# A fused attention + two-MLP kernel: the small products of each tile gathered behind h, scores three tiles ahead, and one weight conversion moved to a later stage

## Chip, cores, metric

The kernel runs on one core of one Trainium2 chip. The metric is the device time of one execution in microseconds; smaller is better. TensorE is called PE here, its weight loads PEld, VectorE DVE, ScalarE ACT, GpSimd POOL, and the queue from which most transfers are issued SP.

## Reference

All inputs are float64 or float32 arrays; the output is float32, 4608 x 512.

```python
# attention in chunks of 64 tokens, 8 heads of 64, 4608 tokens in all
attn = softmax(q_c @ k_c.T / 8)            # per chunk and head, 64 x 64
x = attn @ v_c                             # -> [4608, 512]
# first MLP, d_ff 1024
h = x @ w_in
sm = softmax(h)
solu = h * sm
ln = (solu - mean(solu)) / sqrt(var(solu) + 1e-6) * g_ln
y = ln @ w_out                             # -> [4608, 512]
# second MLP, d_ff 1536
g, val = y @ w_gate, y @ w_val
out = (g * sigmoid(g) * val) @ w_out2
```

## The kernel before

The weights arrive as float64 and are turned into float32 pairs (high and low part) on the chip, by a chain called here a conversion: `conv_a` (ACT takes the magnitude from the upper words), `conv_r` (ACT scales the lower words), `clamp` (POOL), `conv_b` (two DVE operations on the bits) and `conv_c` (POOL adds). Products with float32 accuracy are three passes over such pairs.

The program is three stages behind each other on PE.

**Attention and h (the slots).** The 4608 tokens are 36 tiles of 128. Slot t of `for t in range(NT): slot(t)` computes the 24 matmuls of `hidden(t)` (h = x @ w_in for tile t, 128x512 each, tile `h` in PSUM), in six blocks of four called `h(0)` to `h(5)`. Between the blocks stand the steps of neighbouring tiles: `scores(t + 2)` and `pv(t + 1)` (32 small 64x64 matmuls each by the profile's count, both into the PSUM tile `so_ps`), `p_transpose(t + 1)` (4 transposes into `pt` and an ACT copy), `x_split(t + 1)` (ACT writes the high part of x, DVE the low part), the softmax steps `s_*`, the softmax and normalisation over h of tile t - 1 (`ln_max`, `ln_exp`, `ln_mul`, `ln_sq`), and of tile t - 2 `ln_norm` on POOL and `ln_T` (8 transposes into `tr`, ACT copies, a store to DRAM). Everything is written in program order; each engine works through its own instructions in that order, and a waiting instruction holds up all behind it on its engine. `wo_step(t, i)` fits conversions in: w_out is 8 units and w_out2 is 12, and unit u begins in slot u * 5 // 3, so 20 units lie in 36 slots. Its load is issued at the end of one slot, and its `conv_a`, `conv_r` and `clamp` stand in the next slot, the clamp ahead of `ln_norm` on POOL. `l_load` and `l_split` fetch the normalised tiles back for the next stage.

**y.** `y_run` multiplies by w_out, while `w_tick` converts w_gate and w_val.

**Gate/value products and the last product.** 72 calls of `step(s, f)`, each 42 matmuls of 128x384 (seven products into the PSUM tiles pa to pd), with ACT, DVE and POOL combining the results, then the product with w_out2, whose converted float32 form was stored in `wo_dram` and is read by `t_load`.

Of the kernel before, what the change touches and what calls it, by code (L numbers as in the profile page):

```python
# [8 lines left out]
F32 = mybir.dt.float32  # L9
# [3 lines left out]
I64 = mybir.dt.int64  # L13
# [4 lines left out]
P = 128  # L18
# [5 lines left out]
def attn_moe_moe2_kernel(  # L24
# [13 lines left out]
    nc = tc.nc  # L38
    NT = qT.shape[0]
# [6 lines left out]
    KF = DF // P  # L46
    FT = w_gate.shape[0]
# [66 lines left out]
    def conv_b(cs):  # L114

        for c in cs:
            shift(c)
        for c in cs:
            sign(c)
        return cs  # L120

    def conv_c(c, out=None):

        m, words = c
        if out is None:
# [9 lines left out]
        c, f = divmod(u, KF // 2)  # L135
        return 2 * f, slice(c * DM // 2, (c + 1) * DM // 2)

    def split_scaled(wB, u, w):

        f0, cols = wo_unit(u)  # L140
        for j in range(2):
            f, x = f0 + j, w[:, j * DM // 2:(j + 1) * DM // 2]
            g, hi, lo = g_sb[:, f:f + 1], wB[:, f, 0, cols], wB[:, f, 1, cols]
            nc.scalar.activation(out=hi, in_=x, func=AF.Copy, scale=g)
            nc.vector.scalar_tensor_tensor(
                out=lo, in0=x, scalar=g, in1=hi.bitcast(F32), op0=ALU.mult, op1=ALU.subtract
            )
# [5 lines left out]
    NY = 3 * KF  # L153
# [79 lines left out]
    with ExitStack() as ph1:  # L233
# [92 lines left out]
        def p_transpose(t):  # L326
            e = st.pop(t).rearrange("p (n c) j -> p n (c j)", c=2)
            pt = ps_t.tile([P, H, CH], F32, tag="t", name="pt")
            for n in range(NP):
                nc.tensor.transpose(pt[:, 2 * n:2 * n + 2].rearrange("p h i -> p (h i)"), e[:, n], ident)  # L330
            p = att.tile([P, H, CH], F32, tag="p", name="p")
# [175 lines left out]
        def shf(k):  # L507
            shift(ca[k])
# [50 lines left out]
        add(3)  # L559
        clp(POOL, 4)  # L560
        p_transpose(0)
        scores(1)
        shf(4)
        rnd(4)
# [27 lines left out]
        clp(POOL, 7)  # L592
        add(6)
        p_transpose(1)
        shf(7)
        rnd(7)
        high(6)
# [15 lines left out]
        raws, cs, lows = {}, {}, {}

        NCV = KF + FT
        cv_at = [u * 5 // 3 for u in range(NCV)]

        def wo_step(t, i):

            for u in range(NCV):  # L620
                if cv_at[u] + i != t:
                    continue
                if i == 0:
                    raws[u] = wo_raw(u) if u < KF else raw_load(stage, w_out2[u - KF])
                elif i == 1:
                    cs[u] = conv_a(stage, raws.pop(u))
                    conv_r(cs[u])
                    clamp(nc.gpsimd, cs[u])
                elif i == 2:
                    conv_b([cs[u]])  # L630
                    conv_c(cs[u])
                elif u < KF:
                    split_scaled(wB, u, cs.pop(u)[0])
                else:
                    nc.sync.dma_start(out=wo_dram[u - KF], in_=cs.pop(u)[0])

        def slot(t):


            S = NH // 6  # L640
            new, nxt, old, out = (
                x if 0 <= x < NT else None for x in (t + 2, t + 1 if t else NT, t - 1, t - 2)
            )
            do = lambda x, *fns: [fn(x) for fn in fns if x is not None]
            h = lambda i: t and hidden(t, i * S, (i + 1) * S)
            h(0)
            if t in lows:
                lows.pop(t)()
            h(1)
            do(old, ln_exp)  # L650
            do(new, scores)
            do(nxt, p_transpose)
            do(new, s_max)
            h(2)
            wo_step(t, 1)
            do(out, ln_norm)
            do(old, ln_rec)
            do(new, s_sub)
            do(old, ln_mul)
            h(3)  # L660
            do(new, s_exp)
            if nxt is not None:
# [6 lines left out]
            h(4)  # L669
            do(new, s_rec)  # L670
            do(old, ln_sq)
            wo_step(t, 3)
            h(5)
# [10 lines left out]
            if t in (NT - 3, NT - 2):  # L684
                l_split()

        lraw, lsplit = [], []

# [31 lines left out]
        ln_norm(t - 1)  # L720
# [23 lines left out]
    with ExitStack() as ph2:  # L744
# [200 lines left out]
        def t_load(p):  # L945
# [3 lines left out]
            for j, dst in enumerate((x[:, 1:8:6], x[:, 2:7:4])):  # L949
                nc.sync.dma_start(  # L950
                    out=dst, in_=wo_dram[2 * p + j].rearrange("p (b n) -> p b n", b=2)
                )

        def t_sums(p):
# [61 lines left out]
        for s in range(NSG):  # L1016
            for n, f in enumerate([*range(RING, FT), *range(RING)] if s == 0 else range(FT)):
                late = n + FT * (s - NSG + 2)
                if s == 0 and n in (2, 4, 6):
                    cache_load(n // 2 - 1)  # L1020
                if s + 1 < NSG:
                    if n == (s == 0):
                        y_load(s + 1)
                    if n == (4 if s == 0 else 1):
                        todo = y_units(s + 1)
                if late == 7:
                    t_load(0)
                    t_load(1)
                if 8 <= late < 8 + 2 * NFP and late % 2 == 0:
                    t_sums(late // 2 - 4)  # L1030
                if late in (20, 21):
                    x_load(late - 20)
                step(s, f)
                k = -(-len(todo) // ((FT if s < NSG - 2 else 7) - n)) if todo else 0
                for x in todo[:k]:
                    x()
                todo = todo[k:]
                if 8 <= late < 8 + 2 * NFP and late % 2:
                    t_split(late // 2 - 4)
# [100 lines left out]
```

## Time and profile before

| | us |
|---|---|
| median of 3 runs | 1446.99 (1446.33 to 1447.7) |
| profiled execution, its own time | 1449.33 |
| its span, first to last instruction | 1447.5 |
| PE busy | 1340.7 (93%) |
| DVE, ACT, POOL busy | 978.8 (68%), 625.5 (43%), 429.6 (30%) |

A row of the timeline gives the start, the time covered, the engine, the line, the operation with its output and inputs, the count, and in brackets the idle time of the engine just before with what ended it. "PEclk 1.00" is the full granted clock of PE, 2.4 GHz; 0.5 would be 1.2 GHz. Matmuls overlap, so the modelled end of one run lies a little behind the start of the next.

### The profile page before, as it was taken

To read this page: it belongs to the slowest core of one execution; us is meant where nothing else is said; L and a number is where in the kernel's file an instruction comes from. 1 tells how busy PE (TensorE), PEld (TensorE's weight loads), DVE (VectorE), ACT (ScalarE), POOL (GpSimd) and SP (SyncE) were. 2 spreads that over 40 slices of the span, in tenths; PEclk is the share of its full clock that TensorE was granted. 3 is DMA by queue.
4 is the path that set the end of the run, shared out by engine and by line. 5 is a ranking of instruction groups with operands and counts; after the bars stand their busy time and mean duration, and the time that the engine had idled before them with its cause. 6 is when DMAs were issued, how large, how long until landed. Compare 5 with 4: busy or idle time off the path is not lost.

```text
span 1447.5 us, 26121 instructions
## 1 busy us (share of the span) xinstructions
PE 1340.7 (93%) x10054; PEld 1264.6 (87%) x10054; DVE 978.8 (68%) x1648; ACT 625.5 (43%) x1000; POOL 429.6 (30%) x578
## 2 busy tenths in 40 slices
PE   4888788878889999999999999999999999999998
PEld 3666666666669999999999999999999989999998
DVE  6767656555553777756776676766777777888775
ACT  5556555544455655533333333333333324333342
POOL 5435434434442344412222221322333101100011
PEclk9999999988999999999999999999999999999999
DMA  5544454545646899989738678585899744444441
GB/s 196 161 139 140 157 164 140 155 155 164 194 140 237 338 358 372 330 332 422 272 118 307 247 257 313 195 304 208 321 329 338 251 145 139 148 135 143 132 133 72
DMA packets 143085, 318.39 MB, mean 220 GB/s; under 512 B 10864, under 2 KB 90736, under 8 KB 135280
## 3 DMA queue, kind: packets, MB, share of 16 engines
q1 hardware_dynamic: 136624, 308.06, 61.3%
q10 hardware_dynamic: 6336, 8.65, 1.7%
q8 instruction: 79, 1.29, 0.4%
q14 instruction: 46, 0.38, 0.1%
HBM read 225.45 MB, written 91.23 MB: 219 GB/s over the span
## 4 chain that ended last, share of the span: by engine, by line
PE 75%; DMA 8%; DVE 5%; POOL 4%; issue 4%; ACT 3%; SPq 1%; POOLq 0%; ACTq 0%; DVEq 0%
PE y L164 14%; PE pa L888 10%; PE pd L888 10%; PE pc L888 9%; PE opa L1068 5%; PE opc L1068 5%; PE opb L1068 5%; PE h L372 5%; DMA raw<-in_moe_w_out 5%; PE pb L888 5%; PE tr L453 3%; PE opd L1068 3%; POOL so L441 2%; DVE nm L383 1%; PE so_ps L260 1%
## 5 line engine op out<-in xcount | busy, mean ns | idle before, releaser
L372 PE MATMUL h<-wA,x 128*128 128x512 f32 x864 | 234.5, 422 | 6.3 <-DVE se L395 3.5
L372 PEld LDWEIGHTS h<-wA,x 128*128 128x128 f32 x864 | 169.5, 204 | 43.5 <-DVE se L395 4.2
L164 PE MATMUL y<-lnT,wB 128*128 128x384 f32 x1152 | 201.7, 336 | 0.0
L164 PEld LDWEIGHTS y<-lnT,wB 128*128 128x128 f32 x1152 | 201.2, 189 | 0.0
L921 POOL TENSOR_TENSOR u<-u,p 128x384 f32<-128x384 f32 x72 | 73.1, 1016 | 398.8 <-DVE u L920 391.2
L923 ACT ACTIVATE u<-pa 128x384 f32<-128x384 f32 x72 | 35.5, 492 | 175.3 <-PE pa L888 142.6
L1078 POOL TENSOR_TENSOR work<-work 128x256 f32<-128x256 f32 x36 | 26.4, 744 | 255.6 <-DVE work L1078 255.6
L453 PE MATMUL tr<-ident,so 128*128 128x128 f32 x288 | 47.5, 318 | 56.7 <-POOL so L441 56.7
L453 PEld LDWEIGHTS tr<-ident,so 128*128 128x128 f32 x288 | 37.7, 162 | 61.0 <-POOL so L441 59.7
L383 DVE TENSOR_REDUCE nm<-h 128x1 f32<-128x1024 f32 x36 | 43.9, 1220 | 65.1 <-PE h L372 65.1
L924 DVE TENSOR_TENSOR u<-pa,u 128x384 f32<-128x384 f32 x72 | 40.1, 557 | 70.3 <-ACT u L923 70.2
L1004 ACT ACTIVATE hl<-ry 128x1792 fp32r<-128x1792 f32 x28 | 47.6, 1704 | 78.2 <-PE opd L1068 53.3
L95 POOL TENSOR_SCALAR m<-m 128x512 f32<-128x512 f32 x44 | 38.0, 864 | 140.8 <-ACT m L82 140.8
L928 ACT ACTIVATE u<-p 128x384 f32<-128x384 f32 x72 | 37.9, 526 | 96.7 <-DVE p L927 96.7
L1004 ACT ACTIVATE hl<-work 128x1792 fp32r<-128x1792 f32 x26 | 44.3, 1705 | 80.6 <-PE opd L1068 53.3
L707 DVE TENSOR_TENSOR lnT<-lr,lnT 128x1536 fp32r<-128x1536 f32 x24 | 47.7, 1987 | 39.7 <-ACT lnT L706 36.7
L888 PE MATMUL pd<-ykb,ws 128*128 128x384 f32 x360 | 72.3, 335 | 1.4 <-DVE u L920 1.4
L888 PE MATMUL pa<-ykb,ws 128*128 128x384 f32 x360 | 72.2, 334 | 0.4 <-ACT p L913 0.4
L888 PE MATMUL pc<-ykb,ws 128*128 128x384 f32 x360 | 72.1, 334 | 0.0
L1009 DVE TENSOR_TENSOR hl<-ry,hl 128x1792 fp32r<-128x1792 f32 x28 | 56.5, 2022 | 17.5 <-ACT hl L1004 17.4
L390 ACT ACTIVATE eh<-h,nm 128x1024 f32<-128x1024 f32 x36 | 40.1, 1115 | 62.9 <-DVE nm L383 62.9
L888 PE MATMUL pa<-yka,ws 128*128 128x384 f32 x324 | 65.2, 335 | 1.6 <-ACT p L913 1.6
(141 smaller groups left out, 3247.5 us busy)
## 6 DMA issues: line engine op xcount, KB each, us to landing
ws<-ws SPq DMA_DIRECT2D x57, 1792.0 KB, 8.8
u<-u SPq DMA_DIRECT2D x72, 384.0 KB, 6.8
ln<-lt SPq DMA_DIRECT2D x72, 256.0 KB, 2.7
lr<-ln SPq DMA_DIRECT2D x24, 768.0 KB, 7.2
ry<-u SPq DMA_DIRECT2D x56, 256.0 KB, 3.2
work<-u SPq DMA_DIRECT2D x52, 256.0 KB, 3.2
ws<-shi SPq DMA_DIRECT2D x12, 896.0 KB, 9.9
raw<-in_moe_w_out SPq DMA_DIRECT2D x20, 512.0 KB, 5.0
```

What stands on the lines that cost most here:

```text
L164: nc.tensor.matmul(ys[u], lhsT=wB[:, f, a, d * P:(d + 1) * P], rhs=lnT[m][:, b, f, :], start=(n == 0), stop=(n == NY - 1),)
L372: nc.tensor.matmul(h[:, n * DM:(n + 1) * DM], lhsT=x[:, a, k, :], rhs=wA[:, n * KD + k, b, :], start=(j == 0), stop=(j == NH // 2 - 1),)
L383: nc.vector.tensor_reduce(out=nm, in_=h, axis=AX.X, op=ALU.max, negate=True)
L390: nc.scalar.activation(out=e, in_=h, func=AF.Exp, bias=nm, accum_out=se)
L453: nc.tensor.transpose(tr[:, f, :], so[:, c0:c0 + P], ident)
L707: nc.vector.tensor_tensor(out=lo, in0=x, in1=hi.bitcast(F32), op=ALU.subtract)
L888: nc.tensor.matmul(ps, lhsT=w[:, a, kk * P:(kk + 1) * P], rhs=y[:, b, kk], start=(first and n == 0), stop=(n == 5), skip_group_check=True,)
L921: nc.gpsimd.tensor_tensor(out=u3, in0=u3, in1=p5, op=ALU.add)
L924: nc.vector.tensor_tensor(out=sa, in0=psA, in1=sa, op=ALU.mult)
L1004: nc.scalar.activation(out=hl[n][:, 0], in_=xs[n][:, 1:8], func=AF.Copy)
L1009: nc.vector.tensor_tensor(out=hl[n][:, 1], in0=xs.pop(n)[:, 1:8], in1=hl[n][:, 0].bitcast(F32), op=ALU.subtract,)
L1068: nc.tensor.matmul(acc[g, i, t][:, half], lhsT=hl[n][:, a, j, i * P:(i + 1) * P], rhs=tw[p][:, j, b], start=(p == x == half == 0), stop=(p ...
```

## The change

A slot keeps its work and gets another order. `scores` runs three tiles ahead (`ahead`, t + 3) in place of two, and stands with `pv` and `ln_T` in one block behind `h(5)`; only the 4 transposes of `p_transpose` stay inside h, behind `h(1)`. The ACT copy of `p_transpose` becomes a step of its own (`p_copy`). `ln_max`, `ln_rs` and the low part of x move to other places. w_out's 8 units begin every fourth slot, and the magnitude step stands two slots behind the load. The 12 units of w_out2 leave the slots: as 24 half units of 128x256 they run beside the first 51 calls of `step`. (`NCV` in the diff is `KF + FT`, 20, and `cv_at[u]` is `u * 5 // 3`.)

```diff
 def wo_step(t, name):
-    for u in range(NCV):
-        if cv_at[u] + i != t:
+    for u in range(KF):
+        if t - 4 * u != {"load": 0, "mag": 2, "clamp": 3, "bits": 4, "add": 4, "high": 6, "low": 6}[name]:
             continue
...
 def slot(t):
+    ahead, new, nxt, old, out = at(t + 3), at(t + 2), at(t + 1), at(t - 1), at(t - 2)
+    if t == 0:
+        scores(2)
+        load_qk(4)
+        nxt = None
     h(0)
-    if t in lows:
-        lows.pop(t)()
+    do(nxt, s_mul)
+    do(out, ln_rs)
+    do(old, ln_max)
     h(1)
-    do(old, ln_exp)
-    do(new, scores)
+    do(out, ln_norm)
+    do(new, s_max)
     do(nxt, p_transpose)
-    do(new, s_max)
     h(2)
-    wo_step(t, 1)
-    do(out, ln_norm)
-    do(old, ln_rec)
+    do(old, ln_exp)
     do(new, s_sub)
-    do(old, ln_mul)
+    do(nxt, p_copy)
+    wo_step(t, "bits")
     h(3)
     do(new, s_exp)
-    if nxt is not None:
-        pv(nxt)
-        lows[nxt] = x_split(nxt)
-    do(out, ln_T)
-    wo_step(t, 2)
-    do(old, ln_mu)
-    do(new, s_sum)
+    do(old, ln_rec)
     h(4)
-    do(new, s_rec)
-    do(old, ln_sq)
-    wo_step(t, 3)
+    wo_step(t, "high")
+    do(old, ln_mul)
+    do(new, s_sum)
+    wo_step(t, "clamp")
     h(5)
-    do(new, s_mul)
-    ln_max(t)
-    do(old, ln_rs)
-    if t + 4 < NT:
-        load_qk(t + 4)
-    if t + 3 < NT:
-        load_v(t + 3)
-    wo_step(t, 0)
+    do(nxt, pv)
+    do(new, s_rec)
+    do(old, ln_mu)
+    wo_step(t, "low")
+    if t in (NT - 3, NT - 1):
+        l_split()
+    wo_step(t, "mag")
+    do(ahead, scores)
+    if nxt is not None:
+        x_split(nxt)()
+    do(out, ln_T)
+    do(old, ln_sq)
+    wo_step(t, "add")
+    do(at(t + 5), load_qk)
+    do(at(t + 3), load_v)
+    wo_step(t, "load")
...
 # behind the slots, t = NT - 1
+ln_rs(t - 1)
+ln_max(t)
+ln_norm(t - 1)
 ln_exp(t)
+y_run(wB, 0, NY // 2, ps_h, p2p, ("h",))
...
-ln_T(t - 1)
-y_run(wB, 0, NY, ps_h, p2p, ("h",))
+ln_T(t - 1)
...
 l_split()
+y_run(wB, NY // 2, NY, ps_h, p2p, ("h",))
...
 # gate/value products: 24 half units of w_out2, G = n + FT * s
+if G % 2 == 0 and 0 <= G // 2 - 2 < 2 * FT:
+    v_store(G // 2 - 2)
 step(s, f)
+if G % 2 and 0 <= G // 2 - 1 < 2 * FT:
+    v_bits(G // 2 - 1)
+if G % 2 == 0 and 0 <= G // 2 - 1 < 2 * FT:
+    v_mag(G // 2 - 1)
+if G % 2 and G // 2 < 2 * FT:
+    v_load(G // 2)
```

`v_load` is one SP transfer of 256 KB into `vraw`, `v_mag` is `conv_a`, `conv_r` and `clamp` into `vm`, `v_bits` is `conv_b` and `conv_c`, and `v_store` sends 128 KB to `wo_dram`.

On PE, in the middle of the slots, one slot of before reads as follows, from one slot's h to the next (`so_ps<-kt,qt` are scores, `so_ps<-p,vt` are pv).

```order
L372 MATMUL h<-wA,x 128x512 x16
L260 MATMUL so_ps<-kt,qt 64x64 x16
L330 MATMUL pt<-ident,e 128x128 x4
L372 MATMUL h<-wA,x 128x512 x8
L260 MATMUL so_ps<-p,vt 64x64 x16
L453 MATMUL tr<-ident,so 128x128 x8
L372 MATMUL h<-wA,x 128x512 x16
```

The same place in the changed kernel:

```order
L381 MATMUL h<-wA,x 128x512 x8
L335 MATMUL pt<-ident,e 128x128 x4
L381 MATMUL h<-wA,x 128x512 x16
L265 MATMUL so_ps<-p,vt 64x64 x16
L265 MATMUL so_ps<-kt,qt 64x64 x16
L462 MATMUL tr<-ident,so 128x128 x8
L381 MATMUL h<-wA,x 128x512 x8
```

The instructions of a slot are the same; h is cut once in place of twice (the 16 of before are the last 8 of one tile and the first 8 of the next), and the two 64x64 products now stand next to each other.

On ACT, a slot of before with a conversion reads from the exponential over h (`eh,se`) to the copies of `tr`; `m` and `raw` are the conversion.

```order
L390 ACTIVATE eh,se<-h,nm 128x1024
L332 ACTIVATE p<-pt 128x512
L82 ACTIVATE m<-raw 128x512
L88 ACTIVATE raw<-raw 128x512
L295 ACTIVATE e<-e 128x512
L352 ACTIVATE x<-so_ps 128x512
L455 ACTIVATE lt<-tr 128x512 x2
L419 ACTIVATE eh,sq<-so,nmu 128x1024
```

In the changed kernel a slot with the most conversion work on ACT reads:

```order
L399 ACTIVATE eh,se<-h,nm 128x1024
L341 ACTIVATE p<-pt 128x512
L300 ACTIVATE e<-e 128x512
L146 ACTIVATE wB<-m,g_sb 128x256 x2
L82 ACTIVATE m<-raw 128x512
L88 ACTIVATE raw<-raw 128x512
L361 ACTIVATE x<-so_ps 128x512
L464 ACTIVATE lt<-tr 128x512 x2
L428 ACTIVATE eh,sq<-so,nmu 128x1024
```

The conversion still stands ahead of the high part of x (`x<-so_ps`), but the raw block that it reads was asked for two slots earlier, and the clamp on POOL that follows it stands behind the next slot's `ln_norm`.

In the gate/value products, ACT of the changed kernel reads, at the end of a step with a magnitude and the start of the next (`u<-pa` and `u<-p` are the two sigmoids, `p<-pa` frees the first product's PSUM tile for the fifth):

```order
L939 ACTIVATE u<-pa 128x384
L944 ACTIVATE u<-p_7646 128x384
L82 ACTIVATE vm<-vraw 128x256
L88 ACTIVATE vraw<-vraw 128x256
L820 ACTIVATE ykb<-ry 128x384 x2
L929 ACTIVATE p_7671<-pa 128x384
```

The two new ACT instructions stand between the last sigmoid of one step and the first copy of the next.

## Rows read from the trace of the kernel before

**Rows 1.** Busy time by stretch (us, busy and count per engine, PEclk, DMA, GB/s).

```profile
49.00:425.50 376.50, 307.55 (x3298) 242.79 (x3297) 229.92 (x456) 204.70 (x360) 169.24 (x310) 0.93 0.49 151
...
440.00:631.80 191.80, 191.80 (x1110) 191.80 (x1109) 128.53 (x155) 108.55 (x155) 70.15 (x56) 1.00 0.90 338
631.80:1163.00 531.20, 527.83 (x3036) 524.99 (x3035) 368.18 (x659) 184.04 (x368) 136.77 (x136) 1.00 0.77 278
```

**Rows 2.** Timeline of PE: one whole slot, then the end of the next.

```profile
221.18 3.92 PE L372 MATMUL h<-wA,x 128*128 128x512 f32 x16
225.20 0.69 PE L260 MATMUL so_ps<-kt,qt 64*64 64x64 f32 x32
...
226.24 2.09 PE L372 MATMUL h<-wA,x 128*128 128x512 f32 x8
228.26 0.69 PE L260 MATMUL so_ps<-p,vt 64*64 64x64 f32 x32
228.88 1.09 PE L453 MATMUL tr<-ident,so 128*128 128x128 f32 x8
229.73 3.91 PE L372 MATMUL h<-wA,x 128*128 128x512 f32 x16
...
241.22 1.09 PE L453 MATMUL tr<-ident,so 128*128 128x128 f32 x8 [3.75 <-POOL so L441]
242.07 5.51 PE L372 MATMUL h<-wA,x 128*128 128x512 f32 x16
```

**Rows 3.** All engines in the slot of rows 2 (columns as in rows 1).

```profile
223.42:232.00 8.58, 8.48 (x102) 6.72 (x101) 7.18 (x15) 5.20 (x9) 4.32 (x9) 1.00 0.50 157
```

**Rows 4.** Timeline of PE: slot 2 begins; the last h; behind it.

```profile
48.26 2.09 PE L372 MATMUL h<-wA,x 128*128 128x512 f32 x8 [0.56 <-ACT x L352]
...
423.42 2.11 PE L372 MATMUL h<-wA,x 128*128 128x512 f32 x8
428.78 1.09 PE L453 MATMUL tr<-ident,so 128*128 128x128 f32 x8 [3.25 <-POOL so L441]
```

**Rows 5.** Chain of waits, in time, through one slot with a conversion.

```profile
144.49 4.74 DMA raw<-in_moe_w_out
...
149.25 0.67 ACT m L82
...
150.00 0.62 POOL m L95
150.62 1.18 POOL so L441
```

**Rows 6.** Groups by line, 60 to 420 us: busy, mean ns, idle before.

```profile
L82 ACT ACTIVATE m<-raw 128x512 f32<-128x512 f32 x18 | 12.0, 668 | 37.2 <-DMA raw<-in_moe_w_out 37.2
```

**Rows 7.** Who PE waited for in 49 to 426 us: total, times, longest.

```profile
PE tr L453 <- POOL so L441: 53.4, 19, 4.7
```

**Rows 8.** Timeline of ACT in the same slot: the high part of x.

```profile
229.02 0.60 ACT L352 ACTIVATE x<-so_ps 128x512 fp32r<-128x512 f32 x1 [0.85 <-PE so_ps L260]
```

**Rows 9.** Timeline of ACT, then PE, in a middle step of the gate/value products.

```profile
882.26 0.53 ACT L928 ACTIVATE u<-p 128x384 f32<-128x384 f32 x1 [1.21 <-DVE p L927]
...
884.22 0.49 ACT L913 ACTIVATE p<-pa 128x384 f32<-128x384 f32 x1 [1.03 <-DVE u L932]
...
886.60 1.20 PE L888 MATMUL pa<-yka,ws 128*128 128x384 f32 x6
```

**Rows 10.** Transfers issued in 880 to 1000 us.

```profile
u<-u SPq DMA_DIRECT2D x16, 384.0 KB, 6.4
```

**Rows 11.** Transfers issued in 640 to 700 us: count, KB, median us to landing.

```profile
u<-u SPq DMA_DIRECT2D x8, 384.0 KB, 10.6
```

**Rows 12.** Timeline of ACT, then PE, early in the gate/value products.

```profile
662.52 0.49 ACT L923 ACTIVATE u<-pa 128x384 f32<-128x384 f32 x1 [5.99 <-DMA u<-u]
...
666.33 1.32 PE L888 MATMUL pa<-yka,ws 128*128 128x384 f32 x6 [1.04 <-ACT p L913]
```

**Rows 13.** The page's groups by line: h over the whole span.

```profile
L372 PE MATMUL h<-wA,x 128*128 128x512 f32 x864 | 234.5, 422 | 6.3 <-DVE se L395 3.5
```

More of the change, by code (lines that the diff above doesn't have):

```diff
@@ L136, in wo_unit, with scaled @@
         return 2 * f, slice(c * DM // 2, (c + 1) * DM // 2)
-    def split_scaled(wB, u, w):
+    def scaled(wB, u, w):
         f0, cols = wo_unit(u)
@@ L142, in split_scaled, with split_high, split_low @@
             f, x = f0 + j, w[:, j * DM // 2:(j + 1) * DM // 2]
-            g, hi, lo = g_sb[:, f:f + 1], wB[:, f, 0, cols], wB[:, f, 1, cols]
+            yield x, g_sb[:, f:f + 1], wB[:, f, 0, cols], wB[:, f, 1, cols]
+    def split_high(wB, u, w):
+        for x, g, hi, lo in scaled(wB, u, w):
             nc.scalar.activation(out=hi, in_=x, func=AF.Copy, scale=g)
+    def split_low(wB, u, w):
+        for x, g, hi, lo in scaled(wB, u, w):
             nc.vector.scalar_tensor_tensor(
@@ L330, in p_transpose, with p_copy @@
                 nc.tensor.transpose(pt[:, 2 * n:2 * n + 2].rearrange("p h i -> p (h i)"), e[:, n], ident)
+            st["pt", t] = pt
+        def p_copy(t):
+            pt = st.pop(("pt", t))
             p = att.tile([P, H, CH], F32, tag="p", name="p")
@@ L561, in attn_moe_moe2_kernel @@
         p_transpose(0)
+        p_copy(0)
         scores(1)
@@ L594, in attn_moe_moe2_kernel @@
         p_transpose(1)
+        p_copy(1)
         shf(7)
@@ L612, in attn_moe_moe2_kernel, with wo_step @@
         load_qk(3)
[L613 to L618, printed above, removed]
-            for u in range(NCV):
-                if cv_at[u] + i != t:
+        raws, cs = {}, {}
+        def wo_step(t, name):
+            for u in range(KF):
+                if t - 4 * u != {"load": 0, "mag": 2, "clamp": 3, "bits": 4, "add": 4, "high": 6, "low": 6}[name]:
                     continue
-                if i == 0:
-                    raws[u] = wo_raw(u) if u < KF else raw_load(stage, w_out2[u - KF])
-                elif i == 1:
+                if name == "load":
+                    raws[u] = wo_raw(u)
+                elif name == "mag":
@@ L626, in wo_step @@
                     cs[u] = conv_a(stage, raws.pop(u))
                     conv_r(cs[u])
+                elif name == "clamp":
                     clamp(nc.gpsimd, cs[u])
-                elif i == 2:
+                elif name == "bits":
                     conv_b([cs[u]])
+                elif name == "add":
                     conv_c(cs[u])
-                elif u < KF:
-                    split_scaled(wB, u, cs.pop(u)[0])
+                elif name == "high":
+                    split_high(wB, u, cs[u][0])
@@ L634, in wo_step @@
                 else:
-                    nc.sync.dma_start(out=wo_dram[u - KF], in_=cs.pop(u)[0])
+                    split_low(wB, u, cs.pop(u)[0])
         def slot(t):
             S = NH // 6
-            new, nxt, old, out = (
-                x if 0 <= x < NT else None for x in (t + 2, t + 1 if t else NT, t - 1, t - 2)
-            )
+            at = lambda x: x if 0 <= x < NT else None
+            ahead, new, nxt, old, out = at(t + 3), at(t + 2), at(t + 1), at(t - 1), at(t - 2)
[3 more added lines that the diff above has]
+                nxt = None
@@ L644, in slot @@
             do = lambda x, *fns: [fn(x) for fn in fns if x is not None]
-            h = lambda i: t and hidden(t, i * S, (i + 1) * S)
+            h = lambda i: 0 < t < NT and hidden(t, i * S, (i + 1) * S)
             h(0)
-            if t in lows:
-                lows.pop(t)()
-            h(1)
+            do(nxt, s_mul)
+            do(out, ln_rs)
+            do(old, ln_max)
+            h(1)
+            do(out, ln_norm)
+            do(new, s_max)
+            do(nxt, p_transpose)
+            h(2)
@@ L650, in slot @@
             do(old, ln_exp)
-            do(new, scores)
-            do(nxt, p_transpose)
-            do(new, s_max)
-            h(2)
-            wo_step(t, 1)
-            do(out, ln_norm)
-            do(old, ln_rec)
             do(new, s_sub)
-            do(old, ln_mul)
+            do(nxt, p_copy)
+            wo_step(t, "bits")
             h(3)
             do(new, s_exp)
+            do(old, ln_rec)
+            h(4)
+            wo_step(t, "high")
+            do(old, ln_mul)
+            do(new, s_sum)
@@ L662, in slot @@
+            wo_step(t, "clamp")
+            h(5)
+            do(nxt, pv)
[6 more added lines that the diff above has]
+            do(ahead, scores)
             if nxt is not None:
-                pv(nxt)
-                lows[nxt] = x_split(nxt)
+                x_split(nxt)()
             do(out, ln_T)
-            wo_step(t, 2)
-            do(old, ln_mu)
@@ L668, in slot @@
-            do(new, s_sum)
-            h(4)
-            do(new, s_rec)
-            do(old, ln_sq)
-            wo_step(t, 3)
-            h(5)
-            do(new, s_mul)
-            ln_max(t)
-            do(old, ln_rs)
-            if t + 4 < NT:
-                load_qk(t + 4)
-            if t + 3 < NT:
-                load_v(t + 3)
-            wo_step(t, 0)
+            do(old, ln_sq)
+            wo_step(t, "add")
+            do(at(t + 5), load_qk)
+            do(at(t + 3), load_v)
@@ L682, in slot @@
+            wo_step(t, "load")
             if t in (NT - 6, NT - 5, NT - 4):
                 l_load()
-            if t in (NT - 3, NT - 2):
-                l_split()
         lraw, lsplit = [], []
@@ L719, in attn_moe_moe2_kernel @@
         ln_sq(t)
-        ln_norm(t - 1)
+        ln_T(t - 1)
         ln_rs(t)
-        ln_T(t - 1)
-        y_run(wB, 0, NY, ps_h, p2p, ("h",))
         l_split()
+        y_run(wB, NY // 2, NY, ps_h, p2p, ("h",))
         l_load()
@@ L952, in t_load, with v_load, v_mag, v_bits @@
                 )
+        vw, vc = {}, {}
+        def v_load(u):
+            f, half = divmod(u, 2)
+            vw[u] = cb.tile([P, HC], I64, tag="vraw", name="vraw", bufs=2)
+            nc.sync.dma_start(out=vw[u], in_=w_out2[f][:, half * HC:(half + 1) * HC])
+        def v_mag(u):
+            m = cp.tile([P, HC], F32, tag="vm", name="vm", bufs=2)
+            vc[u] = conv_a(None, vw.pop(u), m)
+            conv_r(vc[u])
+            clamp(nc.gpsimd, vc[u])
+        def v_bits(u):
+            conv_b([vc[u]])
+            conv_c(vc[u])
+        def v_store(u):
+            f, half = divmod(u, 2)
+            nc.sync.dma_start(
+                out=wo_dram[f][:, half * HC:(half + 1) * HC], in_=vc.pop(u)[0]
+            )
         def t_sums(p):
@@ L1018, in attn_moe_moe2_kernel @@
                 late = n + FT * (s - NSG + 2)
+                G = n + FT * s
                 if s == 0 and n in (2, 4, 6):
```

## Prediction

> **What bounds the kernel now.** I first read the busy times by stretch [rows 1]. Behind the slots PE is busy for 191.80 of 191.80 us (y) and for 527.83 of 531.20 us (gate/value products), at the full clock: nothing is to be had there but losses. In the slots it is busy for 307.55 of 376.50 us, at a granted clock of 0.93. So the question is what a slot costs when PE waits for nothing, and what makes it wait.
>
> PE's timeline answers the first [rows 2]. From one h run at 221.18 to the next at 229.73 no row has an idle bracket: a slot without a wait takes 8.55 us, at clock 1.00 [rows 3]. The average is another: slot 2 begins at 48.26 and the last h ends at 423.42 + 2.11 = 425.53 [rows 4], 377.3 us for 34 slots, 11.10 each.
>
> The next slot shows what happens: `tr` waits 3.75 us for POOL's `so`, and the 16 h products behind the gap take 5.51 us in place of 3.92, the clock being at its lower level of 1.2 GHz for part of them (the mean of the whole stretch is 0.93) [rows 1, 2]. The chain of waits tells why POOL is late [rows 5]: the raw block of w_out is issued at 144.49 and takes 4.74 us, ACT takes its magnitude from 149.25, POOL clamps from 150.00, and only then comes `ln_norm` (`so`, 150.62, 1.18 us), for which PE's transposes wait. ACT sat 37.2 us before its 18 magnitudes for that transfer [rows 6], and PE lost 53.4 us to `so` in 19 waits [rows 7], about one for each of the 20 units.
>
> **The slots after the change.** Every instruction of a slot stays, except that 12 of the 20 conversions go. The transfer is issued two slots ahead of the magnitude: 17.1 us at 8.55 each, against 4.74 us [rows 5]; and the clamp stands behind `ln_norm`. So the wait of [rows 5] should be gone, and with it the low clock that followed.
>
> Does a new wait take its place? Engine loads first: in the clean slot DVE is busy 7.18 us, ACT 5.20, POOL 4.32 of 8.58 [rows 3], DVE and POOL with a conversion's work already in it. The heaviest ACT slot adds the magnitude and its twin (0.67 each [rows 6]) and two copies of half that size, about 2.0 us: 7.2 of 8.55. No engine passes PE.
>
> Then the tightest handover, x to h. The high part of x is written by ACT in 0.60 us, and PE fills the time with `tr`. Now: pv starts at 228.26, the high part ends at 229.62 [rows 8], h starts at 229.73 behind `tr` [rows 2]. In the new order scores stands where pv stood, and the high part is written behind it, so the geometry is the same, with 0.11 us to spare. The low part, DVE, is needed only after 8 h products and `pt`. `pt` is asked for 2.02 us into the slot (eight h [rows 2]), and its input `s_mul` is now first on POOL's list. pv comes about 6.5 us in (2.02, some 0.4 for `pt`, 4.02 for sixteen h), with the copy of `pt` issued 4 us before. I take 8.55 us for a slot.
>
> Slots 2 to 34 are then 33 x 8.55 = 282.2 us; the last two of them have no scores (0.62 each, 228.26 to 228.88 [rows 2]): -1.2; the last h is 4.02 + 2.02 = 6.0. One more scores stands ahead of slot 2, +0.6. That makes 287.6 us in place of 377.3: **-89.7**. If nothing but the waits for `so` went it would be -53.4.
>
> The Trainium skill (TensorEngine Tiling (Array Packing), Key Properties) says that a change of the tiling mode drains TensorE; what that would do here is the first of the rivals.
>
> **The end of the slots.** Before, `tr` of tile 34 starts at 428.78, 3.25 us behind the last h [rows 4], and y follows 0.85 us later (as 228.88 to 229.73 [rows 2]), 4.1 us behind that h. After, `tr` of tile 33 stands behind the last h (0.85), then 12 y products (191.8 / 1110 = 0.173 each [rows 1], 2.1 us), then PE waits for tile 34, whose squares ACT takes only after the copies of tile 33's `tr`, roughly 3 us later than before: 6.3 us behind h, plus 0.85. With 2.1 us of y done by then: 7.2 - 2.1 - 4.1 = **+1.0** (from -1 to +3, as the squares come 1 to 5 us later).
>
> **The gate/value products.** 24 half units come in. On ACT each is two instructions of about 0.33 us (half of 0.668 [rows 6]). They are queued behind the second sigmoid, which ends at 882.79, and ahead of the copy that frees pa, which starts at 884.22 since it waits for DVE, and takes 0.49; PE asks for pa at 886.60 [rows 9]. So 3.8 us lie between, of which 0.49 + 0.67 are used: 2.65 us to spare, if the data are there. This is the added wait: behind ACT's magnitude stand that copy and thereby PE's fifth product. The load is issued at the end of the step before, one step earlier, 531.2 / 72 = 7.4 us [rows 1]. Transfers of 384 KB land in 6.4 us in the middle of the stage [rows 10], so 256 KB is there in time. At its start they take 10.6 [rows 11]: 10.6 - 7.4 - 2.65 = 0.55 us lost for each of the first four units, 2 us; there ACT already waits 5.99 us for the stores of u and PE 1.04 for ACT [rows 12], and 4% to 5% more bytes come on top. I take **+4**; the ends are 0 and 24 x 0.55 = 13. The DVE and POOL parts lie beside PE (368 and 137 busy of 531 us [rows 1]). On SP the store of each half unit waits for POOL ahead of the store of u, about 1 us, which takes from the same 2.65.
>
> **Sum**, on the profiled execution's 1449.3: -89.7 + 1.0 + 4 = 1364.6. That execution is 2.3 above the median of the runs, so 1362.3; I say **1362 us**.
>
> **Rivals.**
> *Drains.* h is now cut once in place of twice, and scores follows pv in the same tile shape. Sixteen h products start 4.02 us ahead of the next run [rows 2], while at their own pitch of (3.92 - 0.42) / 15 = 0.233 us [rows 2, 13] they need 3.73: up to 0.29 us may be the change of shape, or the wait for so_ps. Saved once a slot it is 34 x 0.29 = 10 us: 1352, and twice, 1342. Against it: the eight h products ahead of pv take 2.02 against 1.87, only 0.15 more. 12%. The skill's rule above would make it the likeliest; the trace agrees with it only as far as these 0.15 to 0.29 us.
> *The normalisation is late all the same.* `ln_sq`, `ln_rs`, `ln_norm` and `tr` of one tile lie in one slot, one behind the other over ACT, POOL and PE; if PE waits 1 us there in each slot (before, 53.4 / 19 = 2.8 us each time [rows 7]), it is 34 us: 1396. Against it: clean slots run the same chain on POOL without a wait [rows 2]. 14%.
> *The clock.* Scores, pv and `tr` now make one block of 0.62 + 0.62 + 0.85 = 2.1 us without h, where the longest was 1.5. If the clock fell after each, sixteen h products would take 5.51 in place of 3.91 [rows 2], 1.6 a slot: 54 us, 1416. Against it: 1.00 throughout the clean slot [rows 3]. 3%. The Trainium skill (TensorE: Matmul & The Clock Gate, Part 4) says that transposes do not count as busy for the clock, which speaks for this rival; the clean slot's clock speaks against it.
> *Slower.* ACT waits for `vraw` in every half unit. The 84.7 us gained are gone when each of 24 costs 3.5 us, that is when loads of 256 KB land in 7.4 + 2.65 + 3.5 = 13.6 us throughout. The worst stretch has a median of 10.6 for 384 KB [rows 11]. 3% for slower; another 3% for a loss of 20 to 80 us.
> *The change does nothing*: only if the transfer's wait came back at another place in the slot; inside the second rival.
>
> **How the numbers follow.** My forecast has 65% (1350 to 1380). With drains and half of the late normalisation the range is 1344 to 1395; left out are the far end of the drains, the rest of the second rival, the clock and the failing loads, some 15% to 20%. About 0.2% is what a measurement of this kernel can tell from no change. Faster 0.96, same 0.01, slower 0.03.
>
> **What would show it.** Right: starts of the maximum over h 8.5 us apart in all slots; PE waits for `so` near nothing until the last slots; PEclk 1.00 from 49 us on; the slots end near 336 us; the products' stretch 531 to 540 us, with ACT's magnitude of `vm` waiting for DMA only in the first few. Wrong: idle brackets before `tr` or before the first h of a slot; h runs of over 4 us; ACT waiting for `vraw` in the middle of the stage.

## The result, and the profile after the change

The changed kernel takes 1361.48 us (median of 4 runs, 1359.36 to 1362.19), 1447.13 before in the same session: a ratio of 0.9406 [0.939, 0.9422]. The forecast was 1362 us. The total came out, two of its terms didn't. By stage, from the profiled executions (spans 1447.5 and 1359.0 us):

| stretch | before | after | difference | forecast |
|---|---|---|---|---|
| slot 2's h begins | 48.26 | 49.92 | +1.7 | +0.6 |
| slots 2 to 35 (34 slots) | 377.3 | 271.0 | -106.2 | -90.3 |
| last h to first gate/value product | 206.3 | 206.8 | +0.5 | +1.0 |
| gate/value products | 530.1 | 546.4 | +16.3 | +4 |
| last product | 285.6 | 284.9 | -0.7 | 0 |
| span | 1447.5 | 1359.0 | -88.5 | -84.7 |

Busy time by stretch of the changed kernel, with the columns of [rows 1]: the slots, what lies up to the first gate/value product, and the gate/value products.

```profile
49.92:320.94 271.02, 271.02 (x3262) 223.88 (x3263) 220.11 (x432) 184.26 (x334) 148.91 (x286) 1.00 0.59 177
320.94:527.74 206.80, 203.72 (x1178) 203.37 (x1175) 133.52 (x163) 116.53 (x167) 74.85 (x70) 0.99 0.90 331
527.74:1074.11 546.37, 531.37 (x3026) 525.00 (x3025) 376.32 (x706) 196.95 (x415) 167.55 (x184) 1.00 0.78 285
```

The same view of the kernel before, cut exactly at its products:

```profile
631.84:1161.92 530.08, 526.71 (x3025) 523.87 (x3025) 367.21 (x658) 183.53 (x367) 136.77 (x136) 1.00 0.77 278
```

In the slots PE is busy for all of 271.02 us, at clock 1.00 in place of 0.93 [rows 1]; 34 slots take 7.97 us each on average, the last two without scores. In the products PE is now idle for 15.0 of 546.37 us, where it was 3.4 of 530.08. The other 4.7 of the 16.3 us lie in PE's own time (526.71 to 531.37). Of these, 1.7 are a spell at 1.2 GHz that follows a wait of PE, as the row of that wait and the busy times around it show (a clock of 0.83 over 10 us is 1.7 us of full clock lost):

```profile
739.47 2.29 PE L904 MATMUL pa<-yka,ws 128*128 128x384 f32 x6 [1.97 <-ACT p L929]
...
735.00:745.00 10.00, 8.03 (x38) 7.71 (x37) 6.36 (x13) 4.19 (x11) 2.87 (x4) 0.83 0.11 40
```

PE's timeline through one slot of the changed kernel, which answers to [rows 2]:

```profile
106.41 2.10 PE L381 MATMUL h<-wA,x 128*128 128x512 f32 x8
108.35 0.60 PE L335 MATMUL pt<-ident,e 128*128 128x128 f32 x4
108.70 3.91 PE L381 MATMUL h<-wA,x 128*128 128x512 f32 x16
112.54 0.69 PE L265 MATMUL so_ps<-p,vt 64*64 64x64 f32 x32
113.05 0.65 PE L265 MATMUL so_ps<-kt,qt 64*64 64x64 f32 x32
113.63 1.09 PE L462 MATMUL tr<-ident,so 128*128 128x128 f32 x8
114.48 1.86 PE L381 MATMUL h<-wA,x 128*128 128x512 f32 x7
```

The slot takes 114.48 - 106.41 = 8.07 us, not 8.55, and no row has an idle bracket. PE's timeline at both ends of the slots, which answers to [rows 4]:

```profile
49.92 2.12 PE L381 MATMUL h<-wA,x 128*128 128x512 f32 x8 [0.78 <-ACT x L361]
...
320.78 1.03 PE L462 MATMUL tr<-ident,so 128*128 128x128 f32 x8
321.57 2.34 PE L169 MATMUL y<-lnT,wB 128*128 128x384 f32 x12
326.99 1.97 PE L462 MATMUL tr<-ident,so 128*128 128x128 f32 x8 [3.08 <-POOL so L450]
```

The waits for `so` [rows 7] are down to this one at the end. Whom PE waited for in the gate/value products of the changed kernel (total us, times, longest):

```profile
PE pa L904 <- ACT p L929: 11.5, 14, 2.1
PE pd L904 <- DVE u L936: 3.5, 5, 0.8
```

Before, these two waits came to 2.0 us (3 times) and 1.4 us (twice). ACT in the same stretch, with what it waited for:

```profile
ACT u L944 <- DVE p L943: 119.0, 71, 5.3
ACT p L929 <- DVE u L948: 38.5, 44, 1.9
...
ACT vm L82 <- DMA vraw<-in_moe_w_out: 21.1, 15, 3.2
```

Three things are to be seen: ACT waits for the raw block in 15 of 24 half units; it waits 119.0 us for DVE's input of the second sigmoid, where that was 93.6 before; and what it had to spare ahead of the copy that frees pa (the wait for DVE's L948, 67.1 us before) has shrunk to 38.5.

### The profile page after: what moved, and what is told of

Same layout as the page of the kernel before. It is cut to its first block, busy times and chain, and to the rows that moved or that the text cites. A ratio compares the mean times of both kernels' runs of the same rounds, so it can differ in the third digit from the quotient of the medians.

```text
span 1359.0 us, 26290 instructions
## 1 busy us (share of the span) xinstructions
PE 1308.6 (96%) x10054; PEld 1246.0 (92%) x10054; DVE 978.2 (72%) x1672; ACT 619.1 (46%) x1024; POOL 439.9 (32%) x602
## 4 chain that ended last, share of the span: by engine, by line
PE 81%; DMA 7%; DVE 4%; issue 3%; POOL 2%; ACT 2%; SPq 1%; POOLq 0%; ACTq 0%; DVEq 0%
PE y L169 15%; PE h L381 14%; PE pa L904 8%; PE pc L904 7%; PE pd L904 7%; PE opc L1116 6%; PE opb L1116 5%; PE opa L1116 5%; PE pb L904 3%; PE so_ps L265 3%; PE tr L462 3%; PE opd L1116 3%; DMA u<-u 3%; DMA vraw<-in_moe_w_out 2%; PE pt L335 1%
## 5 line engine op out<-in xcount | busy, mean ns | idle before, releaser
L381 PE MATMUL h<-wA,x 128*128 128x512 f32 x864 | 219.9, 403 | 4.1 <-ACT x L361 2.2
L381 PEld LDWEIGHTS h<-wA,x 128*128 128x128 f32 x864 | 158.7, 190 | 37.1 <-ACT x L361 2.5
L937 POOL TENSOR_TENSOR u<-u,p 128x384 f32<-128x384 f32 x72 | 73.0, 1014 | 218.7 <-DVE u L936 209.4
L1048 DVE TENSOR_TENSOR hl<-ry,hl 128x1792 fp32r<-128x1792 f32 x28 | 56.5, 2022 | 16.3 <-ACT hl L1043 16.2
L904 PEld LDWEIGHTS pa<-ykb,ws 128*128 128x128 f32 x360 | 63.0, 188 | 5.2 <-ACT p L929 5.2
L904 PE MATMUL pd<-yka,ws 128*128 128x384 f32 x324 | 65.2, 335 | 1.6 <-DVE u L936 1.6
L904 PE MATMUL pc<-yka,ws 128*128 128x384 f32 x324 | 65.5, 336 | 0.0
L904 PEld LDWEIGHTS pa<-yka,ws 128*128 128x128 f32 x324 | 57.3, 190 | 8.5 <-ACT p L929 8.4
L904 PEld LDWEIGHTS pd<-ykb,ws 128*128 128x128 f32 x360 | 63.1, 188 | 2.1 <-DVE u L936 2.1
```

What stands on the lines that cost most here:

```text
L381: nc.tensor.matmul(h[:, n * DM:(n + 1) * DM], lhsT=x[:, a, k, :], rhs=wA[:, n * KD + k, b, :], start=(j == 0), stop=(j == NH // 2 - 1),)
L904: nc.tensor.matmul(ps, lhsT=w[:, a, kk * P:(kk + 1) * P], rhs=y[:, b, kk], start=(first and n == 0), stop=(n == 5), skip_group_check=True,)
L937: nc.gpsimd.tensor_tensor(out=u3, in0=u3, in1=p5, op=ALU.add)
L1048: nc.vector.tensor_tensor(out=hl[n][:, 1], in0=xs.pop(n)[:, 1:8], in1=hl[n][:, 0].bitcast(F32), op=ALU.subtract,)
```

## The experiments

Times are medians, each with the ratio to the kernel before on the same chip. The kernel before is 1443.9 to 1453.5 us in these runs. "The products" is the stretch from the first gate/value product to the first product with w_out2: 546.4 us in the changed kernel. The times of stages come from one execution of each kernel.

### Where the slots' 106 us came from

**x2_before_early**: the order of before, with the transfer asked for two slots ahead of the magnitude and the clamp behind `ln_norm`.

```diff
-    wo_step(t, 1)              # magnitude, clamp: one slot behind the load
     do(out, ln_norm)
+    wo_step(t, 2)              # two slots behind it, three raw buffers
...
-    wo_step(t, 2)
+    wo_step(t, 3)
...
-    wo_step(t, 3)
+    wo_step(t, 4)
```

> The kernel before with one part of the change alone: the raw block is loaded two slots ahead of its magnitude (three raw buffers), the clamp stands behind the normalisation, and the later conversion steps move one slot on; the order of the products and w_out2's conversion stay. Theory A: the late raw block made almost all of the loss, so slots fall from 11.1 to 8.6 to 8.8 us each and the whole to 1362 to 1372 us. Theory B: the new order of the products is needed as well, since other waits (POOL's normalisation, DVE's low part of x) take the place of the removed one: slots of 9.3 us or more, 1385 us or more.

Measured: 1370.96 us, 0.9456 [0.9435, 0.9476]. The products take 530.0 us, as before. PE's timeline, one slot:

```profile
202.06 3.91 PE L373 MATMUL h<-wA,x 128*128 128x512 f32 x16
206.07 0.69 PE L261 MATMUL so_ps<-kt,qt 64*64 64x64 f32 x32
...
210.58 1.64 PE L373 MATMUL h<-wA,x 128*128 128x512 f32 x6
```

So 8.52 us for the slot of before when no bracket shows a wait, the figure that the prediction read from [rows 2]; the whole is some 78 us faster. In the slots by themselves it is 74 of the 106 us: they take 303.1 us (8.9 each, a little over theory A's 8.8), against 377.3 before and 271.0 in the changed kernel. Of the other 32, some 15 are the slot's own 8.52 against 8.07 us, and 14.1 are waits of PE that the changed order does not have:

```profile
PE so_ps L261 <- DVE x L355: 10.6, 8, 1.5
PE h L373 <- DVE se L396: 3.5, 2, 2.0
```

The late transfer, with the clamp ahead of `ln_norm` behind it, was the main cause of the loss in the slots, as the prediction had it. This run moves the load and the clamp together; which of the two alone would do is not shown.

**x1_split**: the changed kernel, with scores put back inside h, between `h(3)` and `h(4)`.

```diff
     do(old, ln_rec)
+    do(ahead, scores)
     h(4)
...
     wo_step(t, "mag")
-    do(ahead, scores)
```

> The changed kernel with scores of the tile ahead put back inside h, between its fourth and fifth block, away from pv; nothing else changes. A slot of the changed kernel takes 8.07 us, one without an idle bracket of the kernel before 8.55. Theory A: of these 0.48 us about half was a wait of scores for DVE's low part of x, hidden under the modelled end of the h run (in the kernel before scores stood right behind it), and each change of tile shape costs only 0.1 us or so; here that wait cannot come back, so a slot takes 8.2 to 8.3 us and the whole 1365 to 1369 us. Theory B: the two changes of tile shape that come back cost all 0.48 us: 8.5 us a slot, 1376 to 1378 us.

Measured: 1373.58 us, 0.9476 [0.9452, 0.9501]. PE's timeline, one slot:

```profile
201.25 2.10 PE L381 MATMUL h<-wA,x 128*128 128x512 f32 x8
203.18 0.60 PE L335 MATMUL pt<-ident,e 128*128 128x128 f32 x4
203.54 2.09 PE L381 MATMUL h<-wA,x 128*128 128x512 f32 x8
205.56 0.69 PE L265 MATMUL so_ps<-kt,qt 64*64 64x64 f32 x32
206.19 2.11 PE L381 MATMUL h<-wA,x 128*128 128x512 f32 x8
208.23 0.69 PE L265 MATMUL so_ps<-p,vt 64*64 64x64 f32 x32
208.85 1.09 PE L462 MATMUL tr<-ident,so 128*128 128x128 f32 x8
209.70 0.48 PE L381 MATMUL h<-wA,x 128*128 128x512 f32 x1
```

No idle bracket, the same instructions, and 8.45 us: 0.38 more than with one block, and nearer to theory B. The h products in front of a 64x64 block show it: eight take 2.02 and 2.04 us up to scores and pv, and 1.93 up to `pt`; each 64x64 block alone takes 0.62 or 0.63, the two together 0.51 + 0.58. But the edit also cuts h once more.

**x3_cut** tells the cut from the tile shape: `pt`'s four transposes stand as two pairs with four products of h between them.

```diff
     do(new, s_max)
-    do(nxt, p_transpose)
+    p_transpose(nxt, (0, 1))
     h(2)
+    p_transpose(nxt, (2, 3))
```

> The four transposes of a tile into pt stand as two pairs, with four products of h between them: h is cut once more in a slot, but no 64x64 products stand at the new cut. Theory B (each change between products of 64x64 and of 128x128 costs, about 0.2 us each way): the slot stays at 8.07 to 8.15 us, 1361 to 1364 in all. Theory C (each cut of h costs, whatever stands in it): the slot becomes 8.4 to 8.5 us, as with scores inside h (8.45), 1372 to 1375 in all.

Measured: 1365.12 us, 0.9423 [0.9395, 0.9451]. PE's timeline, one slot:

```profile
106.69 2.10 PE L382 MATMUL h<-wA,x 128*128 128x512 f32 x8
108.62 0.38 PE L337 MATMUL pt<-ident,e 128*128 128x128 f32 x2
108.76 1.18 PE L382 MATMUL h<-wA,x 128*128 128x512 f32 x4
...
114.77 2.10 PE L382 MATMUL h<-wA,x 128*128 128x512 f32 x8
```

8.08 us: a cut of h at 128x128 transposes costs no more than 0.01 to 0.02 us. So what x1_split paid is the change to 64x64 products and back. (The median is higher since the products took 551.0 us in this kernel; they lie in nothing that the edit touched, and with half units this stretch was 545.1 to 551.0 us over four kernels.)

### Where the products' 16 us went

**p2_none**: no conversion of w_out2 at all; a constant block is stored during the slots.

```diff
+    if t < FT:
+        nc.sync.dma_start(out=wo_dram[t], in_=zt)
...
-    v_store(G // 2 - 2)
     step(s, f)
-    v_bits(G // 2 - 1)
-    v_mag(G // 2 - 1)
-    v_load(G // 2)
```

> The changed kernel without w_out2's conversion: a constant block is stored to its place during the slots, and the 24 half units are left out of the gate/value products (the output is that of other weights). All theories: if the half units make the whole loss of 16.3 us there, the products take 530 us again and the whole 1344 to 1347 us; if the earlier start of the stage or another order is part of it, the products stay above 533 us.

Measured: 1342.52 us, 0.9257 [0.9236, 0.9277]. Busy time in its products:

```profile
527.91:1059.94 532.03, 527.30 (x3026) 525.54 (x3025) 368.73 (x658) 183.79 (x367) 137.34 (x136) 1.00 0.77 275
```

The half units cost 14.3 of the 16.3 us; the other 2.0 are there without them, and 1.7 of these are again one spell at 1.2 GHz (PEclk 0.83 in 575 to 585 us). By the medians the half units cost 19.0 us (1361.48 to 1342.52): the executions of one kernel differ by several us, and the profiled one, 1346.51, was p2_none's longest of five.

**p1_early**: each load one step earlier.

```diff
-    if G % 2 and G // 2 < 2 * FT:
+    if G % 2 == 0 and G // 2 < 2 * FT:
         v_load(G // 2)
```

> The changed kernel with the load of each half unit of w_out2 issued one step earlier, two steps ahead of its magnitude. The gate/value products take 546.4 us in the changed kernel against 530.1 before. Theory A: ACT's waits for vraw (21.1 us in 15 times) hold up the copy that frees pa; with the load earlier they go and the products take 531 to 536 us, the whole 1347 to 1352 us. Theory B: the work of the half units on POOL, DVE and ACT, and the stores, make the loss: the products stay at 542 us or more, the whole at 1357 us or more.

Measured: 1358.22 us, 0.9369 [0.935, 0.9388]; the products 545.1 us. ACT no longer waits for `vraw`, but for the stores of u in 41.1 us (26.3 in the changed kernel), and PE still loses 14.5 us. So the load's time was not the main price: 1.3 us of the products and 3.3 of the whole came back, and another wait of ACT took the place of the one for `vraw`.

**p4_dma** keeps the transfers without the conversion, **p5_noload** the conversion and the stores without the loads.

```diff
 # p4_dma: neither v_bits nor v_mag
-        in_=vc.pop(u)[0]
+        in_=vz                     # a constant
 # p5_noload
 def v_load(u):
+    if u > 1:
+        vw[u] = vw[u - 2]
+        return
...
 def v_mag(u):
-    vc[u] = conv_a(None, vw.pop(u), m)
+    vc[u] = conv_a(None, vw[u], m)
```

> Left out: the conversion of the 24 half units; their loads (256 KB) and stores (128 KB) stay at their places, and a constant is stored, so the output is that of other weights. The stage of the gate/value products took 546.4 us with the half units and 532.0 without any part of them. Theory T (the transfers cost the time: they hold up the other transfers, u's stores above all, and through them ACT, DVE and PE): 543 to 547 us for the stage, 1358 to 1362 in all. Theory E (the work on ACT, DVE and POOL costs it, queued ahead of what PE waits for): 532 to 535 us, 1343 to 1347 in all. Between them: each has a part.

> Left out: all loads of the 24 half units but the first two; the conversion runs on what lies in the two buffers and is stored as in the changed kernel, so the output is that of other weights. Theory T (the loads cost the time): 532 to 536 us for the stage of the products, 1344 to 1349 in all. Theory E (the work on the engines costs it): 543 to 547 us, 1358 to 1362 in all, PE still waiting about 11 us for the copy of pa.

Measured: p4_dma 1348.79 us, 0.9316 [0.9292, 0.9339], the products 534.3 us; p5_noload 1353.04 us, 0.9353 [0.9333, 0.9372], the products 537.5 us. So by the products of one execution each the transfers alone cost 2.2 us and the work without loads 5.5, but both together 14.3. p4_dma and p5_noload have no spell at 1.2 GHz there; with the 1.7 us taken off the other two it is 4.0, 7.2 and 14.4. By the medians, over p2_none's 1342.52, it is 6.3, 10.5 and 19.0, which nearly add up. Neither theory holds alone; that both together cost more than their sum is not shown.

**p7_nopool** leaves out POOL's two instructions of a half unit, **p8_noact** ACT's two.

```diff
 # p7_nopool
     conv_r(vc[u])
-    clamp(nc.gpsimd, vc[u])
...
     conv_b([vc[u]])
-    conv_c(vc[u])
 # p8_noact: v_mag
-    vc[u] = conv_a(None, vw.pop(u), m)
-    conv_r(vc[u])
-    clamp(nc.gpsimd, vc[u])
+    vc[u] = m, words(vw.pop(u))
+    nc.gpsimd.memset(m, 0.0)
```

> Left out: the two POOL instructions of every half unit (clamp and add); loads, ACT's and DVE's part and the stores stay, so the output is that of other weights. The stage of the gate/value products takes 546.4 us in the changed kernel and 532.0 without half units. Theory P (POOL's add and clamp stand ahead of u3 and of the y sums on POOL, DVE waits for u3's input to come free and passes the delay on to ACT): 533 to 537 us, 1346 to 1351 in all. Theory A (ACT's two instructions, with their wait for the load, hold up the copy of pa): 542 to 546 us, 1357 to 1362 in all.

> Left out: the two ACT instructions of every half unit; POOL writes zeros in place of the clamp and adds another word of the raw block, DVE's part, loads and stores stay, so the output is that of other weights. Theory P (POOL): 542 to 546 us for the stage of the products, 1357 to 1362 in all. Theory A (ACT): 533 to 537 us, 1346 to 1351 in all.

Measured: p7_nopool 1353.49 us, 0.9346 [0.9319, 0.9373], the products 538.2 us; p8_noact 1360.33 us, 0.9386 [0.9359, 0.9413], the products 547.8 us. Busy time in the products of p7_nopool:

```profile
525.09:1063.26 538.17, 530.34 (x3025) 523.32 (x3025) 380.53 (x706) 196.72 (x415) 136.64 (x136) 1.00 0.81 292
```

This fits theory P, with both stretches a little above its ranges (538.2 against 537, 547.8 against 546). Without ACT's two instructions, which the prediction worried about, nothing is gained in the products. Without POOL's two the products are 8.2 us shorter, 6.5 with the changed kernel's spell at 1.2 GHz taken off; the medians say 8.0 of the 19.0. In p7_nopool ACT waits even longer for `vraw`, 32.1 us in 18 times, and PE's waits for pa are still down from 11.5 to 5.3 us. Whom DVE waited for in the products shows one way of it. In the changed kernel:

```profile
DVE p L943 <- POOL u L937: 26.4, 27, 3.3
```

And in p7_nopool:

```profile
DVE p L943 <- POOL u L937: 12.7, 18, 0.7
```

L943 writes c12, the input of the second sigmoid, into the buffer from which POOL's L937 still reads; POOL reaches L937 late when the add, the clamp or the four y sums (4.2 us) stand ahead of it. DVE passes the delay to ACT, and ACT to PE. (Without half units the same wait is 6.7 us in 15 times, in p2_none.) A second way goes by the y sums themselves, and it makes PE's longest wait in the products. POOL, ACT, then PE in the changed kernel:

```profile
912.36 0.99 POOL L130 TENSOR_TENSOR vm<-vm,vraw 128x256 int32<-128x256 int32 x1 [4.70 <-DVE vm L109]
913.31 4.32 POOL L817 TENSOR_TENSOR ry<-ry 128x384 f32<-128x384 f32 x4
...
914.33 0.52 ACT L820 ACTIVATE ykb<-ry 128x384 fp32r<-128x384 f32 x1 [3.84 <-POOL ry L817]
...
915.29 1.31 PE L904 MATMUL pa<-yka,wc 128*128 128x384 f32 x6 [2.10 <-ACT p L929]
```

The sums stand behind the half unit's add, and ACT's copy that frees pa (L929) stands behind L820. ACT has this wait of 3.8 us in p8_noact too, where PE waits 4.26 us for it, and not in p2_none or p7_nopool. A third way is in the timelines of the changed kernel, here POOL, then DVE, then PE, in one step of the products:

```profile
580.23 0.99 POOL L130 TENSOR_TENSOR vm<-vm,vraw 128x256 int32<-128x256 int32 x1 [3.91 <-DVE vm L109]
...
579.72 0.43 DVE L109 SCALAR_TENSOR_TENSOR vm<-vraw,vm 128x256 int32<-128x256 int32 x1
580.06 1.57 DVE L821 TENSOR_TENSOR ykb<-ry,ykb 128x384 fp32r<-128x384 f32 x2
581.56 0.54 DVE L934 TENSOR_TENSOR p<-pb,p 128x384 f32<-128x384 f32 x1
582.21 0.56 DVE L936 TENSOR_TENSOR u<-pd,p 128x384 f32<-128x384 f32 x1
...
582.82 1.34 PE L904 MATMUL pd<-yka,ws 128*128 128x384 f32 x6 [0.81 <-DVE u L936]
```

DVE's two operations of the half unit end just as POOL's add begins; the two subtractions L821 then take 1.57 us, where one takes 0.55 when POOL is idle; L934 and L936 follow with no gap, and PE waits 0.81 us for L936 to free pd. This way is small: PE's waits for pd are 3.5 us in all, 2.5 in p7_nopool and 1.4 in p2_none.

### A version that beats both

**p6_slots**: the changed order of the slot, all 20 conversions in the slots, three raw buffers, no half units.

```diff
-    for u in range(KF):
-        if t - 4 * u != {..., "high": 6, "low": 6}[name]:
+    for u in range(KF + FT):
+        if t - u * 5 // 3 != {..., "high": 5, "low": 5}[name]:
...
-    raws[u] = wo_raw(u)
+    raws[u] = wo_raw(u) if u < KF else raw_load(stage, w_out2[u - KF], bufs=3)
```

> The changed order of the slot, but all 20 conversions lie in the slots (a unit begins in slot u * 5 // 3, its load two slots ahead of the magnitude, three raw buffers), and no half units beside the products. If the conversions in the slots are free when their load is early (my theory of where the loss of the kernel before came from): slot 8.07 to 8.15 us, products 531 to 533 us, 1344 to 1349 in all, faster than the changed kernel by 13 to 17 us. Rival: ACT, DVE or POOL then hold up PE in the slots with a conversion (as in the order of before with early loads, where PE still waited 17 us): 0.5 to 1 us for each of 20 units, 1354 to 1366.

Measured: 1345.64 us, 0.9301 [0.9283, 0.9318]. Busy time in its slots, then in its products (columns as in [rows 1]):

```profile
48.87:319.90 271.03, 271.02 (x3260) 223.60 (x3260) 235.11 (x456) 197.97 (x358) 178.26 (x309) 1.00 0.69 211
...
528.67:1059.68 531.01, 526.34 (x3025) 523.84 (x3025) 369.77 (x658) 183.79 (x367) 137.77 (x136) 1.00 0.77 275
```

The slots take 271.0 us with 20 conversions and with 8. With an early load, the 12 conversions cost nothing beside h; in the gate/value products they cost 14 us. Moving them there was the part of the change that lost.

## Why the prediction was right, and where it was not

**What held the slots up.** Right: the late raw block, ACT's wait, the clamp ahead of `ln_norm` and the low clock behind it. x2_before_early removes that, with the order of before, and gets 74 of the slots' 106 us. The prediction did not name the rest of PE's waits in the slots (those for DVE's `x` and `se`), and the new order removed them too.

**The slot's own time: mis-sized, 8.55 in place of 8.07 us.** The forecast took the slot of [rows 2] as it stood, as one without a wait, and left the gain from one 64x64 block less to a rival with 12%, of 0.15 to 0.29 us per change (1352, and 1342 for twice that). 33 slots by 0.48 are 15.8 us; the table's row differs from the forecast by 15.9. The 0.48 us have two parts. One is a wait that no bracket shows: sixteen h products ahead of a 64x64 block took 4.02 us there [rows 2] and take 112.54 - 108.70 = 3.84 now. Scores at 225.20 waited for DVE's low part of x, which ended at 225.14 in the kernel before:

```profile
224.46 0.68 DVE L354 TENSOR_TENSOR x<-so_ps,x 128x512 fp32r<-128x512 f32 x1
```

It is so in 30 of 32 slots; the step from the last h product to scores is 0.49 us in the slot shown, and 0.32 and 0.33 in the two slots where the low part ended earlier. So some 0.17 us a slot were a wait, hidden under the modelled end of h; the slot of [rows 2] was not free of waits, and the prediction's "or the wait for so_ps" named it without taking it up. The other 0.3 goes with the change of shape. Where h and not `pt` follows the separate block it is 0.38 (x1_split against the changed kernel): 0.22 in the h products ahead of the blocks and 0.16 in the blocks. The rival's bound looked at the front of the block alone; the way out of the shape and the second block's own start are in the price too. The rule of the Trainium skill that the prediction cited there (TensorEngine Tiling (Array Packing), Key Properties: a change of the tiling mode drains TensorE) was the better guide: the trace agrees, at 0.38 us for going in and out once more, and x3_cut shows that a cut without a change of shape costs 0.01.

**The start and end of the slots.** +1.7 and +0.5 in place of +0.6 and +1.0: at 40.69 PE waits 1.54 us for DVE's `e` ahead of the scores that were moved forward, and slot 2 waits 0.78 us for x (0.56 before [rows 4]), since the first block has no `tr` behind it. The end went as worked out, one 3.08 us wait for `so` with 12 y products ahead of it.

**The gate/value products: the step that failed.** The prediction put +4 there, with 13 as its upper bound, and it was +16.3 (530.1 to 546.4), 14.3 of it from the half units. Two of its sentences fell. "The DVE and POOL parts lie beside PE (368 and 137 busy of 531 us [rows 1])": without POOL's two instructions the products are 8.2 us shorter (p7_nopool). A busy share of 26% says nothing of the order in which POOL reaches `u3` and the y sums, nor of what DVE's operations take beside POOL's. And "256 KB is there in time": the prediction went by the 6.4 us of [rows 10], and ACT waited in 15 half units. Its "4% to 5% more bytes" fits the loads alone; with the stores the stretch moves 155.73 MB in place of 147.11, 5.9% more. The transfers of the changed kernel's products (count, KB, median us from issue to landing):

```profile
vraw<-in_moe_w_out SPq DMA_DIRECT2D x24, 256.0 KB, 7.9
```

In the first units ACT's wait for them did cost, as the prediction had it: 2.89 us of ACT at 554.69, and 1.96 of PE at 555.86. As a whole it was not the main price: with 32.1 us of it in place of 21.1 p7_nopool is faster, and p8_noact, where ACT has neither the wait nor the two instructions, is not. The loads cost 8.9 us together with the rest (546.4 to 537.5; 8.4 by the medians). One answer fits these: ACT's 2.65 us to spare, which the prediction worked out, are used up by several small delays that each alone would fit into them. That is argued and not shown; the split of the remaining 6 us between loads, DVE and ACT is open, since this stretch differed by 5.4 us (545.6 in x1_split, 551.0 in x3_cut) between kernels in which it is the same.

**The total.** Errors of -15 (slots, with their start) and +12 us (products) cancelled to within 4 us of span; the 1362 was right by its main term, and by luck in the last per cent. With the products at +4 the kernel would have taken some 1349 us, less than the forecast's 1350 to 1380.

**Late normalisation, low clock, slower.** None came. PEclk is 1.00 in the slots although pv, scores and `tr` stand in one block from 112.54 to 114.48, 1.9 us without h. The Trainium skill (TensorE: Matmul & The Clock Gate, Part 4), which says that transposes do not count as busy in the same way for the clock, spoke for a fall; here the clock stays at its upper level of 2.4 GHz.

## What to carry to other kernels

Before a conversion is moved out of a stage, ask which wait ends last there: when it is a transfer issued too late, issue it earlier and try the work where it is first: here that was 15.8 us better than moving it (p6_slots, 1345.64 against 1361.48). Price an engine's extra work by what stands behind it in its queue and by whom that is awaited, not by its busy share. Put matmuls of another tile shape next to each other where the order allows it: here that was worth some 0.3 us a slot. And compare start to start: a slot without an idle bracket can still hold a wait.

## What the hardware showed that was not expected

A run of 64x64 products that stands by itself inside a stream of 128x512 ones costs 0.38 us more than the same run behind another of its shape (8.45 against 8.07 us a slot), with no idle bracket: it is hidden in the products' modelled times. One more cut of h at 128x128 transposes costs 0.01 to 0.02 (8.08).

DVE's 128x384 subtraction takes 0.55 us alone and up to 1.11 beside POOL. Its mean over 42 of them in the products, here in the changed kernel:

```profile
L821 DVE TENSOR_TENSOR ykb<-ry,ykb 128x384 fp32r<-128x384 f32 x42 | 26.0, 651 | 7.5 <-ACT ykb L820 7.5
```

And in p2_none, without half units:

```profile
L825 DVE TENSOR_TENSOR ykb<-ry,ykb 128x384 fp32r<-128x384 f32 x42 | 21.7, 551 | 0.0
```

The Trainium skill (SBUF — State Buffer, Who interferes with whom) says that a DVE instruction with two inputs in SBUF contends with a GpSimd instruction that reads SBUF; the trace agrees, and the 100 ns more in the mean are its size here. It moved more than it grew: the three DVE operations L947 to L949 take 125.9 us with half units and 138.1 in p2_none (there L951 to L953).
